# Gated linear attention on one core: the list of steps in another order, q's first piece loaded first, upper weights rounded from another tile

## The chip, the core and the metric

The kernel runs on one core of a Trainium2 chip. The core has five engines that work side by side: TensorE (PE, matrix products; PEld is its loading of weights), VectorE (DVE), ScalarE (ACT), GpSimd (POOL) and SyncE (SP), which here only issues the transfers (DMAs). Each engine takes its own instructions strictly in the order in which they were written, and waits on semaphores for what the others produce. The metric is the device time of one execution in microseconds; lower is better.

## The reference

There are 8 batches, 8 heads, 576 tokens and 64 features a head, so 512 channels. First comes linear attention, then a gated layer:

```
q_s = exp(q - max over features);  q_s = q_s / (sum over features + 1e-9)
k_s = exp(k - max over tokens);    k_s = k_s / (sum over tokens + 1e-9)
kv  = einsum('bhsd,bhse->bhde', k_s, v)
x   = einsum('bhsd,bhde->bhse', q_s, kv)          # tokens x 512 channels
gate = sigmoid(causal convolution of x over 5 tokens, one weight per tap and channel)
val  = x @ w_val
out  = (gate * val) @ w_out
```

## The kernel before

All work on x, gate, val and out is done with channels on the 128 partitions and the 576 tokens along the free axis, so a batch has four blocks of channels (0 to 3). The steps of a batch are: turning q (and for the first two batches k) so that features lie on the partitions (`q_turn`, `k_turn`, on PE; `q_turned` and `k_turned` copy the result out of PSUM); `kv`, the product of k and v, 80 short matmuls; `kv_sums` and `kv_norm`, its division by the sums; `attend b g`, which makes x for half of the blocks, 16 matmuls; `x_high` and `x_low`, which split x into a rounded upper part and the rest; `first`, `tap`, `far` with `near`, the five taps of the convolution; `sigmoid`; `value b m`, one block of val; `gated`, gate times val; `g_high` and `g_low`, the split of that; `project b n`, one block of the output; `copy` and `put`. For batch 0 the convolution of blocks 0 and 1 is done by PE (`conv`, with `conv_rows` and `conv_kv` before it).

`value` and `project` are split products of 24 matmuls of 128 x 288: lower weights by upper x, upper weights by upper x, upper weights by lower x. Weights arrive as 64-bit words and are built in pieces of a slab of 128 columns (slabs 0 to 3 of w_val, 4 to 7 of w_out): `load_words`, then `field`, `scaled`, `signed` make the upper part (tile e), `part` the lower part (tile f), `joined` adds them into f, `w_high` rounds to W hi, `w_low` subtracts to get W lo.

k's softmax has `k_sub` (subtract the maximum, four pieces and a tail) and `k_exp`; from batch 2 on, the maxima come by `load_km`, `k_peak`, `k_row`, `k_spread`. From batch 3 on the softmax of q in the turned form has `l_row` and `l_spread`, by which a row goes to memory and comes back spread over the partitions (tile lb), `l_sub` (subtract it, on tile qc) and `c_exp`.

Nothing but one list sets the order: ORDER, 973 steps written out by hand or by a planner. A loop calls each step in turn, and every engine has its instructions in this order. The last letter of a step names its engine (a ScalarE, p GpSimd, v VectorE) where there is a choice. HOMES gives for each kind of tile the buffer that its next one takes, as a string of digits, so a buffer comes free when the former tile of that digit has been read. All transfers go through SyncE's queue in the order of the list. The lines that matter below: w_high L323 and w_low L326, split_product L621, value L682, attend (matmuls L580), kv (L521), conv (L676), x_low (L600), q_max (L415), q_each (L499), k_sub (L355), k_exp (L359), l_sub (L490), near (L614).

Of the kernel before, what the change touches and what calls it, by code (L numbers as in the profile page):

```python
# [19 lines left out]
NB = C // P  # L20
# [11 lines left out]
    warm 12, load_words 3, field 3 p, load_q 0 2 5, load_kc 0 0, load_q 0 0 1, load_taps, scaled 3 p, signed 3,  # L32
    load_q 0 1 2, q_max 0 2 3, q_sub 0 2 p, q_max 0 3 5, q_sub 0 3 p, part 3 a, joined 3 v, k_top 0 0, load_ident,
    load_words 0, load_kc 0 1, load_kc 0 2, load_kc 0 3, load_words 1, load_v 0, q_max 0 0 1, tap_field p,
    tap_scaled p, tap_signed, load_vt 0, load_km 2 2, q_exp 0 2 3, q_each 0 4, q_exp 0 3 4, q_each 0 0, q_max 0 1 2,
    load_km 2 1, tap_part p, tap_joined p, diag p, q_sub 0 1 p, q_sum 0 2 5, q_eps 0 2 5 p, k_raise 0 0, q_exp 0 1 2,
    k_top 0 1, k_raise 0 1, k_turn 0 0, field 0 p, load_words 2, load_q 1 0 5, load_words 4, load_km 2 0,
    load_words 5, q_rec 0 2 5, k_top 0 2, q_mul 0 4 p, tail_turn 0, k_raise 0 2, k_top 0 3, k_raise 0 3, k_turn 0 1,
    q_sum 0 0 2, q_eps 0 0 2 a, q_mul 0 3 p, q_rec 0 0 2, load_kc 1 3, load_kc 1 0, k_turned 0 1 v, k_turned 0 0 a,
    k_tail_turn 0, k_tail_turned 0 v, q_mul 0 2 p, load_kc 1 1, field 1 p, scaled 0 a, signed 0, scaled 1 a, signed 1,  # L40
    q_mul 0 0 p, part 1 a, q_mul 0 1 a, k_peak 2 2, tail_turned 0 a, conv_rows, tail_high 0 a, joined 1 p, kv 0,
    kv_sums 0, field 2 p, kv_norm 0 v, conv_kv, load_words 7, load_kc 1 2, part 2 a, q_turn 0 0, q_turned 0 0 a,
    scaled 2 p, signed 2, joined 2 p, q_turn 0 1, q_turned 0 1 a, w_high 1 a, q_max 1 0 2, attend 0 0, w_low 1 p,
    x_high 0 1 a, x_low 0 1, x_high 0 0 a, q_sub 1 1 p, x_low 0 0, q_max 1 2 4, attend 0 1, first 0 2 a, load_words 6,
    x_high 0 3 a, load_v 1, first 0 3 a, tap 0 3 3, w_high 3 p, tap 0 3 1, part 0 a, x_high 0 2 a, field 4 p,
# [758 lines left out]
```

## Time and profile before

| | us |
|---|---|
| median of 3 runs | 287.61 (287.55 to 287.83) |
| the profiled execution | 287.65 |
| its span, first to last instruction | 285.9 |
| PE busy in it | 278.8 |
| VectorE, GpSimd, ScalarE busy | 231.7, 205.8, 192.8 |
| granted clock of PE | 1.00 of full speed throughout |

The profile comes from one execution, whose own time lies 1.75 us above its span. Times in the rows are microseconds from the first instruction. A busy time counts the instructions alone; an engine that is not busy waits, and the profile names what ended the wait.

### The profile page before, as it was taken

The page shows a single profiled execution, that of the slowest core. Times are in us where ns is not written, and L with a number is a line of the kernel's source. Part 1 is how long each engine was busy: PE and PEld are TensorE (multiplying, and loading weights), DVE is VectorE, ACT ScalarE, POOL GpSimd, SP SyncE. Part 2 cuts the span into 40 slices and gives each one's busy share as a digit, 9 for nine tenths or more (in the row PEclk, how much of TensorE's full clock was granted, in tenths as well). Part 3 has the DMA queues.
Part 4 walks back from the last instruction along what each step waited for, and adds up shares of the span by engine and source line. Part 5 has one row for each costly group of instructions (what it writes and reads, how often), then busy time and mean ns, then how long its engine had stood idle before and what let it go on. Part 6 is the DMA issues. An engine that isn't in the chain of part 4 may idle for free.

```text
span 285.9 us, 6653 instructions
## 1 busy us (share of the span) xinstructions
PE 278.8 (98%) x2640; PEld 250.6 (88%) x2640; DVE 231.7 (81%) x329; ACT 192.8 (67%) x322; POOL 205.8 (72%) x191
## 2 busy tenths in 40 slices
...
GB/s 241 397 414 399 316 226 301 214 416 346 84 262 345 250 284 128 332 198 224 371 417 257 211 225 322 287 165 126 153 182 159 217 0 2 44 41 85 0 83 85
DMA packets 23463, 62.93 MB, mean 220 GB/s; under 512 B 3432, under 2 KB 3976, under 8 KB 20744
## 3 DMA queue, kind: packets, MB, share of 16 engines
...
q8 instruction: 21, 0.34, 0.5%
q14 instruction: 10, 0.08, 0.1%
...
## 4 chain that ended last, share of the span: by engine, by line
PE 84%; DVE 7%; ACT 2%; issue 1%; POOL 1%; DVEq 0%
PE val L630 36%; PE out_a L630 32%; PE kv L521 6%; PE x L580 5%; PE cv L676 2%; DVE gate L605 2%; DVE x L600 1%; PE qTps L546 1%; DVE e L292 1%; DVE kpk L340 1%; PE kps L387 1%; ACT q L506 1%; PE out_r L630 1%; PE out_l L630 1%; POOL f L295 0%
## 5 line engine op out<-in xcount | busy, mean ns | idle before, releaser
L630 PE MATMUL val<-x,w_val_hi 128*128 128x288 f32 x512 | 89.1, 295 | 0.1
L605 DVE SCALAR_TENSOR_TENSOR gate<-x,cw,gate 128x575 f32<-128x575 f32 (+3 forms) x98 | 78.8, 809 | 5.7 <-ACT gate L593 2.2
L630 PEld LDWEIGHTS val<-x,w_val_hi 128*128 128x128 f32 x512 | 75.3, 188 | 0.3 <-DVE x L600 0.3
L630 PE MATMUL val<-x,w_val_lo 128*128 128x288 f32 x256 | 56.1, 300 | 0.0
L630 PE MATMUL out_a<-gh,w_out_lo 128*128 128x288 f32 x248 | 54.6, 301 | 0.0
L630 PE MATMUL out_a<-gh,w_out_hi 128*128 128x288 f32 x248 | 53.2, 296 | 0.0
L697 POOL TENSOR_TENSOR gl<-g,gh 128x576 fp32r<-128x576 f32 x24 | 34.6, 1443 | 14.7 <-ACT gh L198 8.0
L630 PEld LDWEIGHTS out_a<-gh,w_out_lo 128*128 128x128 f32 x248 | 39.4, 188 | 5.7 <-issue 1.8
L630 PE MATMUL out_a<-gl,w_out_hi 128*128 128x288 f32 x248 | 43.0, 295 | 0.0
L614 POOL TENSOR_TENSOR gate<-gate,far 128x572 f32<-128x572 f32 (+3 forms) x22 | 29.1, 1324 | 18.7 <-DVE gate L605 10.0
L630 PEld LDWEIGHTS val<-x,w_val_lo 128*128 128x128 f32 x256 | 40.7, 188 | 1.6 <-DVE g L689 0.4
L630 PEld LDWEIGHTS out_a<-gh,w_out_hi 128*128 128x128 f32 x248 | 39.8, 188 | 0.0
L204 ACT ACTIVATE o<-out_a 128x576 f32<-128x576 f32 x27 | 17.6, 650 | 31.6 <-PE out_a L630 22.0
L630 PEld LDWEIGHTS out_a<-gl,w_out_hi 128*128 128x128 f32 x248 | 36.4, 188 | 0.0
L420 POOL TENSOR_TENSOR q<-q,qm 128x512 f32<-128x512 f32 x32 | 33.5, 1062 | 3.6 <-DVE qm L415 3.5
L689 DVE SCALAR_TENSOR_TENSOR g<-gate,val 128x576 f32<-128x576 f32 x32 | 23.8, 749 | 13.8 <-PE val L630 5.9
L490 POOL TENSOR_TENSOR qc<-qc,lb 128x576 f32<-128x576 f32 (+1 forms) x17 | 24.1, 1428 | 11.0 <-DMA lb<-lrow 11.0
L355 POOL TENSOR_TENSOR k<-k,kmax 128x512 f32<-128x512 f32 x23 | 30.2, 1330 | 0.2
L617 ACT ACTIVATE gate<-gate 128x576 f32<-128x576 f32 x30 | 20.2, 683 | 8.3 <-DVE gate L605 8.0
L600 DVE TENSOR_TENSOR x<-x,x 128x576 fp32r<-128x576 f32 x32 | 23.1, 749 | 1.7 <-ACT x L198 1.6
L610 ACT ACTIVATE far<-x,cw 128x572 f32<-128x572 f32 (+3 forms) x22 | 16.2, 737 | 9.2 <-PE x L580 4.0
L424 ACT ACTIVATE q<-q 128x512 f32<-128x512 f32 (+2 forms) x11 | 15.9, 1442 | 8.8 <-POOL q L420 8.8
(108 smaller groups left out, 456.4 us busy)
## 6 DMA issues: line engine op xcount, KB each, us to landing
...
```

The costliest lines, as they stand in the source:

```text
L204: nc.scalar.mul(out, in_, factor)
L355: engine(e).tensor_sub(kk[r, cs], kk[r, cs], mx[r, cs])
L420: engine(e).tensor_tensor(qq, qq, m, op=ALU.add if b < 2 else ALU.subtract)
L490: engine(e).tensor_sub(t, t, T["lb", b][:, p])
L521: nc.tensor.matmul(acc[h * D:(h + 1) * D, p, :], T["k", b][:, c, cs] if c < 4 else ktz[b % 2][:, cs], T["v", b][:, c, hd] if c < 4 else T[ ...
L600: nc.vector.tensor_sub(xl, T["x", b, p], T["xh", b, p].bitcast(F32))
L605: nc.vector.scalar_tensor_tensor(out=a, in0=x, scalar=w, in1=a, op0=ALU.mult, op1=ALU.add)
L614: nc.gpsimd.tensor_add(a, a, T["far", b, p, j])
L617: nc.scalar.activation(T["gate", b, p], T["gate", b, p], AF.Tanh, scale=0.5)
L630: nc.tensor.matmul(ps[:, cs], a[:, kb, ms], z[:, cs], start=(i == 0), stop=(i == len(parts) - 1))
L689: nc.vector.scalar_tensor_tensor(out=T["g", b, m], in0=T["gate", b, m], scalar=1.0, in1=T["val", b, m], op0=ALU.add, op1=ALU.mult)
L697: engine(e).tensor_sub(T["gl", b, m], T["g", b, m], T["gh", b, m].bitcast(F32))
```

## The change

The list is written in another order, 96 of its steps go to another engine, and the buffers in HOMES are dealt anew. Both products of k and v of batches 6 and 7 stand next to an attention half. The first transfer is q's tokens 2 and 3 with the tail instead of the weights' slab 3, whose load comes later; `warm` has 11 matmuls for 12. `conv_rows` follows `warm` more closely. `w_high` rounds the upper part e of a weight, where it rounded the joined f. For batch 0 `value` takes the matmuls of the upper weights first, those of the lower weights last. By the steps' letters VectorE, ScalarE and GpSimd trade subtractions of q, k, lb and the lower g, conversions of weights and roundings; the set of matmuls, taps and transfers is the same. In the diff the lists are cut to the lines where the named steps stand.

```diff
     def w_high(i, e="a"):
-        copied(e, W[i // NB][0][:, :, slab(i)], weights(i))
+        copied(e, W[i // NB][0][:, :, slab(i)], T["e", i].rearrange("p (k c) -> p k c", k=NB))
...
-    def split_product(ps, w, hi, lo, m, order, last=0, h="a"):
+    def split_product(ps, w, hi, lo, m, order, last=0, h="a", early=False):
...
         for ks in (order[:NB - last], order[NB - last:]):
-            parts += [(w, hi[kb], kb) for kb in ks for w in (wl, wh)] + [(wh, lo[kb], kb) for kb in ks]
+            if early:
+                parts += [(wh, z[kb], kb) for z in (hi, lo) for kb in ks] + [(wl, hi[kb], kb) for kb in ks]
+            else:
+                parts += [(w, hi[kb], kb) for kb in ks for w in (wl, wh)] + [(wh, lo[kb], kb) for kb in ks]
...
-        split_product(T["val", b, m], W[0], blocks("xh", b), blocks("xl", b), m, T["split", b])
+        split_product(T["val", b, m], W[0], blocks("xh", b), blocks("xl", b), m, T["split", b], early=b == 0)
...
-    sigmoid 5 2, g_low 5 1 v, put 4 1, g_high 5 0 a, load_qc 7 1, kv 6, gated 5 2, sigmoid 5 3, l_sub 6 1 v,
-    g_high 6 1 p, gated 6 3, g_low 6 1 p, tap 6 2 1, c_exp 7 2, tap 6 2 0, g_high 6 3 p, c_exp 7 1, l_sub 7 0 p, kv 7,
-    value 7 3, gated 7 0, g_high 7 0 p, g_low 7 0 v, gated 7 3, g_high 7 3 v, g_low 7 3 v, project 7 0, project 7 1,
-    copy 7 0 a v, put 7 0, project 7 2, copy 7 1 a a, put 7 1, project 7 3 r, copy 7 2 a a, put 7 2, project 7 3 l,
...
+    tap 5 1 0, far 5 0 3, tap 5 1 2, project 4 0, load_qc 6 0, put 3 2, k_exp 6, near 5 0 3, copy 4 0 a a, attend 5 1,
+    x_high 5 2 a, x_high 5 3 v, first 5 2 a, near 5 0 0, k_peak 7 1, load_qc 7 1, first 5 3 a, far 5 2 2, q_total 6,
+    load_vt 6, kv 6, kv_sums 6, load_k 7, far 5 2 3, kv_norm 6 v, near 5 2 2, q_log 6, l_turn 6, tap 5 3 0,
+    c_exp 6 2, kv 7, l_sub 6 3 p, c_exp 6 3, tap 6 1 3, sigmoid 6 1, kv_sums 7, l_spread 7, l_sub 7 3 p, put 5 1,
+    project 7 1, copy 7 1 a a, put 7 1, project 7 3 r, copy 7 3 r v, put 7 3 r, project 7 0, copy 7 0 a a, put 7 0,
+    project 7 3 l, copy 7 3 l a, put 7 3 l,
```

SyncE's first transfers before (tile and its number, source, shape):

```order
L265 DMA words3_108<-in_w_val 128x1024
L236 DMA q0_112<-in_q 128x1024
L238 DMA q0_112<-in_q_tail 128x512
L370 DMA kc_0_0_115<-in_k_channels 128x576
L236 DMA q0_112<-in_q 128x512
L298 DMA tap_words_74<-in_conv_w 128x40
```

And SyncE's first transfers in the changed kernel:

```order
L236 DMA q0_107<-in_q 128x1024
L238 DMA q0_107<-in_q_tail 128x512
L370 DMA kc_0_0_112<-in_k_channels 128x576
L236 DMA q0_107<-in_q 128x512
L298 DMA tap_words_74<-in_conv_w 128x40
L236 DMA q0_107<-in_q 128x512
```

The slab of weights no longer stands ahead of q, and its 512 KB come after k's channels and the tail of v.

ScalarE around the end of the head before, from k's first turned copy to the first rounding of x (k0 and qT are the turned k and q, f the lower part of a weight, x2 the pair that holds x's split):

```order
L198 COPY k0_237<-kps_0_0_188 128x4x256
L204 ACTIVATE e0_197<-e0_197 128x512
L204 ACTIVATE e1_249<-e1_249 128x512
L204 ACTIVATE f1_258<-words1_142 128x512
L506 ACTIVATE q0_112<-q0_112,qs_0_181 128x64 x8
L198 COPY qTt_0_270<-qTtps_0_212 128x512
L198 COPY qT_0_277<-qTt_0_270 128x4x64
L204 ACTIVATE f2_333<-words2_199 128x512
L198 COPY qT_0_277<-qTps_0_0_335 128x2x512
L198 COPY qT_0_277<-qTps_0_1_349 128x2x512
L198 CAST w_val_hi_77<-f1_258 128x4x128
L198 CAST x2_0_1_373<-x_0_1_363 128x576
```

The same stretch of ScalarE in the changed kernel (ktz is the turned tail of k):

```order
L198 COPY k0_232<-kps_0_1_220 128x4x256
L198 COPY qT_0_244<-qTt_0_216 128x4x64
L198 COPY ktz0_83<-ktps_0_246 64x512
L198 COPY k0_232<-kps_0_0_234 128x4x256
L506 ACTIVATE q0_107<-q0_107,qs_0_176 128x64 x8
L204 ACTIVATE f1_327<-words1_127 128x512
L198 CAST w_val_hi_77<-e3_303 128x4x128
L204 ACTIVATE f2_340<-words2_165 128x512
L198 COPY qT_0_244<-qTps_0_0_329 128x2x512
L204 ACTIVATE f3_369<-words3_148 128x512
L198 COPY qT_0_244<-qTps_0_1_346 128x2x512
L198 CAST x2_0_1_385<-x_0_1_360 128x576
```

ScalarE now has both of k's turned copies and the tail's, and rounds slab 3 from its upper part e3 ahead of q's turned copies; one scaled step (e1) has left it.

GpSimd around the subtractions of k of batch 6 before (k6 and kt6 are k and its tail, qc with lb the subtraction that needs the spread row, gh and gl the split of gate times val):

```order
L490 TENSOR_TENSOR qc_5_3_2136<-qc_5_3_2136,lb5_2210 128x576
L697 TENSOR_TENSOR gl_4_2_2504<-g_4_2_2462,gh_4_2_2501 128x576
L200 CAST gh_4_1_2535<-g_4_1_2531 128x576
L697 TENSOR_TENSOR gl_4_1_2539<-g_4_1_2531,gh_4_1_2535 128x576
L614 TENSOR_TENSOR gate_5_0_2545<-gate_5_0_2545,far_5_0_3_2547 128x575
L614 TENSOR_TENSOR gate_5_0_2545<-gate_5_0_2545,far_5_0_0_2578 128x572
L355 TENSOR_TENSOR k6_2445<-k6_2445,kmax_6_2447 128x512 x2
L614 TENSOR_TENSOR gate_5_2_2631<-gate_5_2_2631,far_5_2_3_2635 128x575
L420 TENSOR_TENSOR q7_2492<-q7_2492,qm_7_2639 128x512 x4
L614 TENSOR_TENSOR gate_5_2_2631<-gate_5_2_2631,far_5_2_2_2667 128x574
L355 TENSOR_TENSOR k6_2445<-k6_2445,kmax_6_2447 128x512 x2
L355 TENSOR_TENSOR kt6_2390<-kt6_2390,kmax_6_2447 64x512
```

And GpSimd there in the changed kernel:

```order
L490 TENSOR_TENSOR qc_5_1_2088<-qc_5_1_2088,lb5_2268 128x576
L355 TENSOR_TENSOR k6_2078<-k6_2078,kmax_6_2381 128x512
L355 TENSOR_TENSOR kt6_2392<-kt6_2392,kmax_6_2381 64x512
L490 TENSOR_TENSOR qc_5_2_2398<-qc_5_2_2398,lb5_2268 128x576
L355 TENSOR_TENSOR k6_2078<-k6_2078,kmax_6_2381 128x512
L490 TENSOR_TENSOR qc_5_3_2429<-qc_5_3_2429,lb5_2268 128x576
L200 CAST gh_4_2_2466<-g_4_2_2464 128x576
L700 TENSOR_TENSOR gl_4_2_2499<-g_4_2_2464,gh_4_2_2466 128x576
L355 TENSOR_TENSOR k6_2078<-k6_2078,kmax_6_2381 128x512
L200 CAST gh_4_1_2510<-g_4_1_2505 128x576
L700 TENSOR_TENSOR gl_4_1_2512<-g_4_1_2505,gh_4_1_2510 128x576
L355 TENSOR_TENSOR k6_2078<-k6_2078,kmax_6_2381 128x512
```

The five subtractions of batch 6's k moved ahead of the near taps of batch 5 and in among the three that use lb.

## Rows read from the trace of the kernel before

**Rows 1.** The page's first section: busy us, share of span, instructions.
```profile
PE 278.8 (98%) x2640; PEld 250.6 (88%) x2640; DVE 231.7 (81%) x329; ACT 192.8 (67%) x322; POOL 205.8 (72%) x191
```

**Rows 2.** Waits of PE, the largest: total us, times, longest.
```profile
PE cv L676 <- DVE x L600: 1.1, 1, 1.1
```

**Rows 3.** Stretch 8.64:25.10: length, PE, PEld, DVE, ACT, POOL busy, clock, DMA.
```profile
8.64:25.10 16.46, 14.82 (x158) 9.01 (x156) 14.89 (x26) 16.25 (x42) 12.69 (x17) 1.00 1.03 410
```

**Rows 4.** Timeline of the head: start, us, engine, line, out<-in, count, [wait].
```profile
4.29 0.67 ACT L204 ACTIVATE f<-words 128x512 int32<-128x512 uint32 x1 [2.29 <-DMA words<-in_w_val]
...
6.80 1.80 DVE L415 TENSOR_REDUCE qm<-q 128x8 f32<-128x512 f32 x2
...
8.64 0.63 ACT L424 ACTIVATE q<-q 128x512 f32<-128x512 f32 x1 [3.68 <-POOL q L420]
...
25.50 1.19 ACT L198 CAST x<-x 128x576 fp32r<-128x576 f32 x2
25.54 1.21 DVE L415 TENSOR_REDUCE qm<-q 128x16 f32<-128x1024 f32 x1
...
26.67 1.41 DVE L600 TENSOR_TENSOR x<-x,x 128x576 fp32r<-128x576 f32 x2
...
27.47 5.73 PE L676 MATMUL cv<-qT,dg 64*64 64x288 f32 x80 [1.07 <-DVE x L600]
```

**Rows 5.** Chain of waits: start, us, engine and line.
```profile
17.18 0.90 ACT k L198
...
19.25 0.58 ACT f L204
...
42.19 3.44 PE val L630 x24
...
181.16 3.20 PE out_a L630 x24
184.36 1.13 PE x L580 x16
...
253.74 3.39 PE out_a L630 x24
...
282.75 0.41 ACT o L204
```

**Rows 6.** The page's costly groups: value's weight loads, busy, mean ns, idle before.
```profile
L630 PEld LDWEIGHTS val<-x,w_val_hi 128*128 128x128 f32 x512 | 75.3, 188 | 0.3 <-DVE x L600 0.3
```

**Rows 7.** Stretches 28.1:68.7 and 68.7:104.2, columns as in rows 3.
```profile
28.10:68.70 40.60, 40.37 (x417) 35.82 (x416) 39.98 (x58) 36.01 (x80) 33.96 (x34) 1.00 0.85 304
68.70:104.20 35.50, 35.45 (x341) 33.50 (x341) 34.64 (x47) 29.47 (x49) 32.43 (x29) 1.00 0.79 239
```

**Rows 8.** Timeline of VectorE at batch 2's last x_low.
```profile
102.77 1.41 DVE L600 TENSOR_TENSOR x<-x,x 128x576 fp32r<-128x576 f32 x2
```

**Rows 9.** Timelines of VectorE and ScalarE ahead of batch 6's k times v.
```profile
181.28 0.75 DVE L689 SCALAR_TENSOR_TENSOR g<-gate,val 128x576 f32<-128x576 f32 x1 [0.92 <-PE val L630]
...
182.07 0.67 ACT L198 CAST gh<-g 128x576 fp32r<-128x576 f32 x1 [0.80 <-DVE g L689]
...
198.41 1.92 ACT L359 ACTIVATE k<-k 128x2048 f32<-128x2048 f32 x1 [1.26 <-POOL k L355]
```

**Rows 10.** Waits of POOL, the largest: total us, times, longest.
```profile
POOL qc L490 <- DMA lb<-lrow: 11.0, 3, 5.2
```

**Rows 11.** Timelines of VectorE and GpSimd, alone and side by side.
```profile
215.17 4.44 POOL L355 TENSOR_TENSOR k<-k,kmax 128x512 f32<-128x512 f32 x3
215.19 0.75 DVE L490 TENSOR_TENSOR qc<-qc,lb 128x576 f32<-128x576 f32 x1
...
239.75 0.75 DVE L697 TENSOR_TENSOR gl<-g,gh 128x576 fp32r<-128x576 f32 x1
...
265.01 1.43 POOL L697 TENSOR_TENSOR gl<-g,gh 128x576 fp32r<-128x576 f32 x1
265.09 1.97 DVE L697 TENSOR_TENSOR gl<-g,gh 128x576 fp32r<-128x576 f32 x1 [0.77 <-POOL gh L200]
```

More of the change, by code (lines that the diff above doesn't have):

```diff
@@ L31 @@
 ORDER = [step.strip() for step in """
[L32 to L45, printed above, removed]
-    tap 0 3 0, q_each 1 3, conv, field 5 p, x_low 0 3, scaled 5 p, tap 0 3 2, joined 0 p, w_high 0 p, w_low 0 p,
@@ L137 @@
[L137 to L139 removed]
+    warm 11, load_q 0 2 5, q_max 0 2 3, load_kc 0 0, q_sub 0 2 p, load_q 0 0 1, load_taps, load_q 0 1 2, load_ident,
+    load_kc 0 1, load_words 0, load_kc 0 2, load_kc 0 3, load_words 1, tap_field p, load_v 0, load_vt 0, q_max 0 3 5,
@@ new lines @@
+    tap 1 0 1, joined 6 p, w_high 6 a, load_km 5 2, q_sub 2 2 p, project 0 1, copy 0 1 a a, put 0 1, part 7 a,
+    tap 1 1 0, tap 1 0 0, tap 1 0 3, w_low 6 p, k_spread 2, project 0 0, copy 0 0 a a, q_sub 2 4 p, tap 1 1 3,
+    attend 1 1, first 1 3 a, x_high 1 3 a, q_sub 2 3 p, x_high 1 2 a, project 0 2, x_low 1 1, q_sub 2 1 p, tap 1 1 1,
+    tap 1 1 2, signed 7, sigmoid 1 1, w_high 7 p, far 1 2 2, joined 7 p, q_sub 2 0 v, load_km 3 3, first 1 2 a,
+    x_low 1 3, x_low 1 2, w_low 7 p, tap 1 3 2, k_sub 2 1 p, value 1 0, k_sub 2 3 p, tap 1 2 3, k_sub 2 4 p, put 0 0,
@@ new lines @@
+    q_sub 5 1 p, project 2 2, copy 2 2 a a, attend 3 1, far 3 3 1, x_high 3 2 v, l_row 4, k_sub 4 3 v, x_high 3 3 a,
+    first 3 2 a, tap 3 2 3, q_sub 5 3 p, put 2 1, first 3 3 a, x_low 3 3, x_low 3 2, tap 3 2 2, project 2 3,
+    value 3 0, k_exp 4, copy 2 3 a a, kt_exp 4, kv 4, near 3 3 1, q_sub 5 2 p, tap 3 3 0, tap 3 3 2, far 3 2 1,
+    tap 3 2 0, sigmoid 3 0, gated 3 0, tap 3 3 3, value 3 2, q_sub 5 0 p, load_qc 4 0, q_exp 5 0 4, q_total 5,
+    q_log 5, k_row 5, k_peak 6 3, k_peak 7 0, near 3 2 1, sigmoid 3 2, g_high 3 0 p, g_low 3 0 p, sigmoid 3 1,
@@ new lines @@
+    x_high 4 0 a, l_sub 4 2 v, tap 4 1 3, c_exp 4 2, project 3 3, k_sub 5 0 p, x_low 4 0, x_high 4 1 a, tap 4 0 3,
+    x_low 4 1, c_exp 4 3, kt_exp 5, q_max 6 0 5, k_sub 5 1 p, copy 3 3 a a, project 3 1, copy 3 1 a a, near 4 1 0,
+    tap 4 0 0, k_exp 5, attend 4 1, x_high 4 3 a, first 4 2 v, tap 4 2 2, tap 4 2 0, x_high 4 2 a, x_low 4 2,
+    l_spread 5, tap 4 2 1, near 4 1 1, x_low 4 3, project 3 2, q_sub 6 1 p, q_sub 6 4 p, q_sub 6 0 p, value 4 0,
+    q_sub 6 3 p, put 3 3, q_sub 6 2 v, load_qc 5 0, copy 3 2 a a, tap 4 2 3, l_sub 5 0 v, sigmoid 4 0, kv 5,
```

198 lines of the change are left out of this document (97 added, 101 removed).

## Prediction

> **What bounds the kernel now.** I read the page first: TensorE (PE) is busy 278.8 of 285.9 us, the next engine, VectorE, 231.7 [rows 1]. Then the waits of PE: the largest is 1.1 us, once, for VectorE's subtraction that splits x into its upper and lower part (L600) [rows 2]. Then the timeline of the head: from 27.47 on the convolution runs, its main part once that wait is over at about 28.1 (x_low of the first two blocks runs from 26.67 to 28.08) [rows 4]. Behind it PE stands almost without a gap up to 282.72, where the copy of the last product begins [rows 5]. So the matmuls, of which the change has the same set, set the time between 28.1 and 282.7, and an edit can act in four places only: how early the convolution starts; how long a product takes beside its neighbours; the small waits inside; the last microseconds. The two engines that feed PE are nearly full at the start: ScalarE is busy 16.25 of 16.46 us between 8.64 and 25.10 [rows 3], VectorE 39.98 of 40.60 in the stretch behind it [rows 7]. Only later is there slack.
>
> **The head.** Before, the first load is a slab of weights (512 KB); q's tokens 2 and 3 come second and q's tail third. The weights are used at 4.29, when they have landed, and the maxima of the q that came behind them begin at 6.80 [rows 4]: 768 KB more in 2.5 us, some 300 GB/s. ScalarE's first exponential of q starts at 8.64 [rows 4]. After, q's 512 KB go first and will be there at about 4.3, the tail's 256 KB 0.85 later, at 5.15. One maximum over two pieces takes 1.21 [rows 4], so ScalarE can start on the tail at about 6.4, 2.2 us earlier, without the subtraction on GpSimd in between.
>
> But ScalarE has more to do from there to the end of q's last turned copy (q_turned 0 1; before it ended the stretch of [rows 3], at 25.1). New ahead of it are k's turned copy of the other half (0.90, the row of such a copy [rows 5]), two part steps (2 x 0.58 [rows 5]), the rounding of an upper weight (bounded by the same 0.58; it reads and writes as much), the turned tail of k (as much again) and two tiny ones, put at 0.27; one scaled step leaves, priced by the part's 0.58. The sum is 0.90 + 1.16 + 0.58 + 0.58 + 0.27 - 0.58 = 2.9. ScalarE was full, so this comes on top: q_turned 0 1 ends at 25.1 - 2.2 + 2.9 = 25.8. Its two roundings of x take 1.19 together [rows 4], so they end at 27.0. The subtraction of the first block then starts at about 26.4 rather than 26.67, once VectorE's maximum of batch 1 (25.54, 1.21 [rows 4]) is done; that maximum gets free of the weight step that stood ahead of it, by about 0.6, so it ends at 26.1 and does not decide. The second subtraction starts at 27.05 and ends at 27.75, against 28.08. I take -0.4. At best ScalarE's additions hide elsewhere and VectorE's maximum decides, which is 0.6 earlier: -0.6. At worst the tail comes late and only 1.2 of the 2.2 are there: q_turned 0 1 ends at 26.8, the second subtraction at 28.7, so +0.6.
>
> The granted clock is 1.00 in the head, with PE busy 14.82 of 16.46 [rows 3]. The new head gives PE no pause that I work out as longer than 1.6 us (18 to 19.5, k's copies), so I put nothing on the clock.
>
> **The seams.** A product (24 matmuls) takes 3.20 behind another product, and 3.39 to 3.44 behind an attention half, a k times v or a turn of q or k: the chain of waits has the first such at 42.19 and the last at 253.74, and a plain one at 181.16 [rows 5]. By the written order there are 23 such places before and 21 after: k times v of batches 1, 6 and 7 move next to another short piece (-3), and k's turn of batch 1 is split by a product (+1). That is 2 x 0.19 = 0.4. What a seam between k times v and an attention half costs isn't seen in the trace before; it lies between nothing and the 0.19 of the seam that goes. I take nothing, so -0.4, with bounds of 0 and -0.6.
>
> **The wait inside.** Weight loads of the value products wait 0.3 us for x_low in one place, value of batch 1 [rows 6]. Between x_low of the last block of batch 0 and the one that is waited for, VectorE has by the rows of its own steps 37.5 us of work after the change, 39.6 before, in a stretch where it is full [rows 7]. So 2 us of slack come, and the wait goes: -0.3.
>
> **The upper weights rounded early.** w_high reads the upper part directly, so it need not wait for the join. For batch 0 the matmuls with the lower weights come last, 2.1 us (16 of 24 matmuls of a 3.20 product) behind the first. In the rows of PE's waits no weight stands ahead of x_low [rows 2, 6], so there is nothing to give back: nothing. What covers it is that the matmuls with the new W lo now come last; were w_high late instead, its product would wait, which the same rows don't bound.
>
> **Batches 6 and 7.** k times v of batch 6 goes some 20 us earlier. What it needs is k_exp 6, which stood at 198.41 for 1.92 [rows 9], right ahead of the old place. In the new order ScalarE comes to it behind the rounding of g of batch 4's last block and one far tap: that block's g began at 181.28 and took 0.75 [rows 9]. PE is 0.7 ahead there by the head and the wait inside, so g ends at 181.3, the rounding (0.67) and far (priced by the same 0.67 [rows 9]) at 182.65, and k_exp at 184.6. PE comes to the new place, behind a product (3.20) and an attention half (1.13) that began at 181.16 [rows 5]: 181.16 - 0.7 + 4.3 = 184.8. So there is no margin; if the far tap's own input or GpSimd's subtraction before k_exp is late, the wait is up to the 1.26 that k_exp waited for GpSimd before [rows 9]. Between 0 and 1.3 I take 0.4. v's tail and k come by DMA with about as little to spare. For batch 7 the gap is some 4 us between the last load and its use: nothing.
>
> **Engines.** 96 steps change their engine. By the durations of each step's rows VectorE gets 7 us more, ScalarE 5.5 more, GpSimd 25 less. VectorE's 231.7 [rows 1] become some 239 of 286, still behind PE's; it costs only where VectorE is full [rows 7], which is rival B.
>
> **The tail.** The last products change places but the last one to be copied is the same left half of block 3 (0.41 at 282.75 [rows 5]), with one 288 KB store more in the queue ahead of it, started 1.4 us earlier: nothing, at most 0.2.
>
> **The sum**: -0.4 (head) - 0.4 (seams) - 0.3 (wait) + 0.4 (batch 6) = -0.7 on the profiled execution's 287.65 (span 285.9 and 1.75 around it), which is 0.04 over the median 287.61 of the runs. That gives 286.9.
>
> **One rule of the skill against this.** VectorE's subtraction of the lower g took 0.75 at 239.75 while GpSimd was idle, but 1.97 at 265.09 when GpSimd had one of 1.43 since 265.01; yet at 215.19 one took 0.75 beside GpSimd's three that began at 215.17 and took 1.48 each [rows 11]. The Trainium skill, "GPSIMD Engine Reference", section "8. Key points", says that GpSimd shares its SBUF interfaces with VectorE and that it contends with VectorE instructions that have two SBUF inputs. The first pair agrees, the second only in that GpSimd's is the one that is stretched. By that rule the 15 steps with two such inputs that VectorE gets would be paid for twice where both engines work.
>
> **The rivals.**
> A. *The head gives nothing*: ScalarE's 2.9 us eat the 2.2, VectorE or GpSimd is late instead. For it: [rows 3], no slack. Against: VectorE's maximum moves up. Without the head's 0.4 the sum is -0.3: 287.35, no change. 0.20.
> B. *VectorE is stretched beside GpSimd*, by up to 1.2 us an instruction as at 265.09 [rows 11]. The place is x_low of batch 2's last blocks, which ends at 104.18 before [rows 8]. From x_low of batch 1 up to there VectorE's steps come to 37.2 us after, 34.7 before, where it is busy 34.64 of 35.50 [rows 7]: 2.5 more, of which 0.9 fits the idle time and the rest waits unless the product has slack there, so 0 to 1.6. I take 0.9: 286.95 + 0.9 = 287.85. Against: GpSimd has 25 us less to disturb it with. 0.15.
> C. *Slower: batch 6's k times v is too early.* k_sub 6 stands on GpSimd behind the step on qc of batch 5 that needs the rows lb from memory; GpSimd waited for these 11.0 us in 3 places before, 5.2 the longest [rows 10]. If that or the load of v's tail is late, k_exp 6 ends late and PE stands with nothing behind it able to pass. It decides once PE's wait passes 1.6, with k_exp 6 ending after 186.4. As its price I take half the longest, 2.6, less the margin of 0.2: 2.4 in place of the 0.4 of the sum, 286.95 + 2.0 = 288.95. 0.17.
> D. *Both terms at their best and nothing given back at batch 6*: 287.65 - 0.6 - 0.6 - 0.3 = 286.15, taken as 286.1. 0.06.
> That the change does not do what it says is left with 0 of weight, since the order of each engine shows it.
>
> **How the numbers follow.** Forecast 0.42, A 0.20, B 0.15, C 0.17, D 0.06. About 0.2% (0.58 us) is what a measurement of this kernel can tell from no change: faster is below 287.03, slower above 288.19. The forecast lies only 0.1 inside, so of its 0.42 I give 0.32 to faster and 0.10 to the same; with D (0.06) and a rest of A and B on the faster side (0.07) faster is 0.45. The same is 0.10 + 0.16 (A) + 0.08 (B) = 0.34; slower is C (0.17) with 0.04 of B = 0.21. The likeliest case's own range is 286.3 to 287.2; the range that should hold 8 in 10 goes from D's 286.1 to within 0.4 of C's, 288.6.
>
> **What would show it.** Right: the convolution's main run starts at 27.5 to 27.9; the weight-load wait for x_low of batch 1 is gone; k times v of batch 6 waits under 1 us for ScalarE; the tail from the last product on takes 3.2. Wrong: a PE wait of more than 1 us behind 28 that has no counterpart before, on k_exp 6 (C) or on x_low of batch 2 (B); a convolution that starts at 28 or later (A).

## The result, and the profile after

The changed kernel is slower: 291.6 us (290.27 to 292.87, 4 runs) against 287.72 for the kernel before in the same comparison, a ratio of 1.0133 (95% interval 1.0105 to 1.0161). Its own runs lie 2.6 us apart, those of the kernel before 0.5. The profiled execution is the slowest of the four: 292.87, span 291.1. The forecast was 286.9, with a range up to 288.6. A ratio, here and in the table of experiments, leaves out runs more than 1.5% above the fastest of their own kernel, while medians and ranges have all runs; the two part clearly only for after_back, where four of six are left out.

First the page, its first section and the row of PE's clock (tenths of full speed in 40 slices), answering [rows 1]:

```profile
PE 281.4 (97%) x2638; PEld 252.2 (87%) x2638; DVE 241.8 (83%) x345; ACT 196.7 (68%) x332; POOL 185.5 (64%) x165
...
PEclk9998999999999999999999999999999999999999
```

PE has 2.6 us more busy time with the same matmuls but one in `warm`, and one slice near the start with less clock. PE's waits (us in total, times, longest), answering [rows 2]:

```profile
PE kv L521 <- ACT k L198: 1.6, 1, 1.6
PE warm L730 <- POOL ones L748: 1.0, 1, 1.0
PE x L580 <- DVE kvd L537: 1.0, 2, 0.7
...
PE out_a L633 <- POOL gl L700: 0.7, 1, 0.7
...
PE val L633 <- DVE x L600: 0.3, 1, 0.3
```

The convolution's wait of 1.1 is gone; four others have come. Where they cost is read by setting each PE step's start against that of the same step before. The changed kernel is late by 1.56 us at the end of the convolution (34.76, before 33.20); by 1.47 at the second attention half of batch 2 (99.39, 97.92); by 4.27 at project 2 1 (126.63, 122.36); by 5.30 at project 3 3 (158.58, 153.28); by 5.61 at the second half of batch 5 (189.90, 184.29); by 5.22 at the end (287.93, 282.71). So there are three places of loss: the head, 97 to 127, and 149 to 175. Behind them the kernel gains.

**The head.** Timeline of PE before and in kv of batch 0:

```profile
17.79 0.60 PE L399 MATMUL ktps<-ident,kc 128*64 128x128 f32 x4
19.97 0.73 PE L521 MATMUL kv<-v,k 128*64 128x65 f32 x16 [1.58 <-ACT k L198]
...
20.70 1.09 PE L521 MATMUL kv<-v,k 128*64 128x65 f32 x16
```

PE stood 1.58 us for ScalarE's second copy of k and began kv 0. Its first 16 matmuls took 0.73, the next 16 took 1.09; before, such 16 took 0.64. The granted clock of the stretch falls (length; PE, PEld, DVE, ACT, POOL busy; clock; DMA):

```profile
18.40:24.10 5.70, 4.13 (x81) 4.07 (x82) 4.25 (x9) 5.09 (x14) 1.85 (x2) 0.70 1.03 406
```

A mean of 0.70 is a mixture of the two levels, 2.4 and 1.2 GHz; kv 0 took 4.13 instead of 2.55. That is as much as the head's 1.56; the rest of the head comes out even, since kv 0 begins 0.42 later than before and the convolution's wait of 1.1 is gone. The matching timeline of ScalarE, VectorE and PE, answering [rows 4]:

```profile
5.00 2.02 DVE L415 TENSOR_REDUCE qm<-q 128x8 f32<-128x512 f32 x2 [5.00 <-DMA q<-in_q]
...
7.06 2.02 ACT L499 ACTIVATE q<-q,qm 128x64 f32<-128x64 f32 x8 [5.05 <-DVE qm L415]
...
17.15 0.99 ACT L198 COPY k<-kps 128x1024 f32<-128x1024 f32 x1
18.43 0.58 ACT L198 COPY ktz<-ktps 64x512 f32<-64x512 f32 x1
18.91 1.00 ACT L198 COPY k<-kps 128x1024 f32<-128x1024 f32 x1
```

q's first piece is there at 5.0, ScalarE starts 1.6 earlier than before (7.06, 8.64), and then has all three of k's copies one behind the other.

**97 to 127.** SyncE's issues of batch 3's row (lrow, lb) and of k of batch 4, before:

```profile
93.82 0.79 SPq L475 DMA_DIRECT2D lrow<-lt  x1
...
97.15 1.33 SPq L486 DMA_DIRECT2D lb<-lrow  x2
...
100.99 0.42 SPq L226 DMA_DIRECT2D k<-in_k  x1
```

and after:

```profile
99.06 0.79 SPq L475 DMA_DIRECT2D lrow<-lt  x1
99.91 0.39 SPq L226 DMA_DIRECT2D k<-in_k  x1
103.47 1.32 SPq L486 DMA_DIRECT2D lb<-lrow  x2
```

The row comes 5 us later, and k's megabyte now stands between its two transfers. The chain of waits from there (start, us, what):

```profile
99.06 4.33 DMA lrow<-lt
...
103.47 8.87 DMA lb<-lrow
...
116.17 1.31 POOL qc L490
...
118.05 0.61 ACT qT L493
118.66 0.59 ACT gate L617
...
119.33 0.75 DVE g L692
120.08 0.23 DVE kvd L537
```

and what GpSimd did meanwhile, with PE's wait behind it:

```profile
107.09 1.41 POOL L614 TENSOR_TENSOR gate<-gate,far 128x572 f32<-128x572 f32 x1
114.93 2.54 POOL L490 TENSOR_TENSOR qc<-qc,lb 128x512 f32<-128x512 f32 x2 [6.43 <-issue]
117.42 2.83 POOL L700 TENSOR_TENSOR gl<-g,gh 128x576 fp32r<-128x576 f32 x2
```
```profile
126.26 0.53 PE L633 MATMUL out_a<-gl,w_out_hi 128*128 128x288 f32 x2 [0.69 <-POOL gl L700]
```

One late transfer holds three queues: GpSimd's first qc stands idle for 6.4 us with g's lower parts behind it, ScalarE's c_exp with a sigmoid behind it, and VectorE's gated with kv_norm behind that. Attention of batch 3 and project 2 0 wait; the latter takes 5.10 instead of 3.47. These two are 1.9 of the 2.8 lost here; 0.66 went earlier, at value 2 1, which waits for x_low.

**149 to 175.** Attention of batch 4 begins 0.7 later still, for kv_norm 4 (kvd). In this execution VectorE does not wait for a transfer ahead of it; it is full. Busy times from batch 3's first attention half to batch 4's (columns as above, VectorE the third after the length), after and before:

```profile
121.77:153.85 32.08, 30.58 (x288) 28.67 (x289) 30.95 (x45) 22.88 (x32) 25.51 (x21) 1.00 0.73 223
```
```profile
119.12:148.85 29.73, 29.73 (x289) 28.56 (x289) 24.42 (x34) 20.91 (x28) 27.55 (x24) 1.00 0.92 295
```

VectorE has 6.5 us more to do there than before, 30.95 of 32.08. Two of its rows after:

```profile
147.02 1.90 DVE L355 TENSOR_TENSOR k<-k,kmax 128x512 f32<-128x512 f32 x1
...
153.28 0.42 DVE L537 TENSOR_TENSOR kvd<-kv,ks 128x256 f32<-128x256 f32 x1
```

The subtraction of k, one of the steps moved to VectorE, stands ahead of kv_norm 4; it took 1.90 here and 0.68 in a second profile (run again below).

**Behind 175 us** the order does what it should. The chain there:

```profile
189.97 1.13 PE x L580 x16
191.10 2.48 PE kv L521 x80
```

kv of batch 6 follows the attention half without a wait. Behind kv 6 and kv 7 the lateness falls from 5.61 to 5.22: two seams of 0.2.

### The profile page after: what moved, and what is told of

Its sections match the earlier page's. It is cut to its first block, busy times and chain, and to the rows that moved or that the text cites. A ratio compares the mean times of both kernels' runs of the same rounds, so it can differ in the third digit from the quotient of the medians.

```text
span 291.1 us, 6636 instructions
## 1 busy us (share of the span) xinstructions
PE 281.4 (97%) x2638; PEld 252.2 (87%) x2638; DVE 241.8 (83%) x345; ACT 196.7 (68%) x332; POOL 185.5 (64%) x165
## 4 chain that ended last, share of the span: by engine, by line
PE 64%; DVE 17%; DMA 7%; ACT 6%; issue 4%; POOL 1%; SPq 0%; DVEq 0%; POOLq 0%; ACTq 0%
PE out_a L633 26%; PE val L633 25%; PE kv L521 6%; DVE gate L605 5%; PE x L580 4%; DMA lb<-lrow 3%; DMA lrow<-lt 2%; DVE qs L449 2%; DVE x L600 2%; PE qTps L546 2%; DVE qm L415 2%; DMA q<-in_q_tail 2%; ACT q L499 1%; DVE k L355 1%; DVE g L692 1%
## 5 line engine op out<-in xcount | busy, mean ns | idle before, releaser
L633 PE MATMUL val<-x,w_val_hi 128*128 128x288 f32 x512 | 87.7, 297 | 0.5 <-DVE x L600 0.3
L605 DVE SCALAR_TENSOR_TENSOR gate<-x,cw,gate 128x573 f32<-128x573 f32 (+3 forms) x98 | 77.8, 809 | 4.2 <-POOL gate L614 1.2
L633 PEld LDWEIGHTS val<-x,w_val_hi 128*128 128x128 f32 x512 | 74.5, 188 | 1.6 <-DVE x L600 0.5
L633 PE MATMUL val<-x,w_val_lo 128*128 128x288 f32 x256 | 53.7, 298 | 0.0
L700 POOL TENSOR_TENSOR gl<-g,gh 128x576 fp32r<-128x576 f32 x20 | 29.5, 1480 | 16.4 <-DVE gh L200 9.5
L420 POOL TENSOR_TENSOR q<-q,qm 128x512 f32<-128x512 f32 x27 | 28.6, 1083 | 9.3 <-DVE qm L415 9.3
L490 POOL TENSOR_TENSOR qc<-qc,lb 128x576 f32<-128x576 f32 (+1 forms) x14 | 19.4, 1402 | 17.4 <-DMA lb<-lrow 9.0
L355 POOL TENSOR_TENSOR k<-k,kmax 128x512 f32<-128x512 f32 x22 | 29.4, 1350 | 0.4 <-DMA kmax<-krow 0.2
L415 DVE TENSOR_REDUCE qm<-q 128x8 f32<-128x512 f32 (+3 forms) x12 | 20.9, 1741 | 5.1 <-DMA q<-in_q 5.0
L593 ACT ACTIVATE gate<-x,cw 128x576 f32<-128x576 f32 x27 | 19.6, 743 | 6.1 <-PE x L580 6.1
```

The lines of the kernel that those rows point to most:

```text
L355: engine(e).tensor_sub(kk[r, cs], kk[r, cs], mx[r, cs])
L415: nc.vector.tensor_reduce(out=T["qm", b][:, cs], in_=qq, axis=AX.X, op=ALU.max, negate=b < 2)
L420: engine(e).tensor_tensor(qq, qq, m, op=ALU.add if b < 2 else ALU.subtract)
L490: engine(e).tensor_sub(t, t, T["lb", b][:, p])
L593: nc.scalar.activation(a, x, AF.Copy, scale=w)
L605: nc.vector.scalar_tensor_tensor(out=a, in0=x, scalar=w, in1=a, op0=ALU.mult, op1=ALU.add)
```

## The experiments

All times are medians in us; the kernel before lay between 287.72 and 287.86 in each comparison. The ratio is to it.

| run | what | median (range) | ratio, 95% interval |
|---|---|---|---|
| again | the changed kernel | 292.06 (290.13 to 294.9) | 1.0148 (1.0112 to 1.0184) |
| lb_first | k's load behind lb | 289.65 (288.69 to 291.1) | 1.0067 (1.0044 to 1.0091) |
| before_k_ahead | before, k's load ahead of lb | 287.88 (287.61 to 288.49) | 1.0005 (0.9996 to 1.0013) |
| before_bunched | the same with more loads behind k_row 3 | 287.85 (287.65 to 288.09) | 1.0000 (0.9991 to 1.0008) |
| norm | lb_first, kv_norm 4 early | 287.82 (287.26 to 291.11) | 1.0023 (0.9997 to 1.0049) |
| puts | lb_first, two stores early | 288.31 (287.93 to 290.56) | 1.0046 (1.0024 to 1.0067) |
| all_three | norm and puts | 288.48 (287.57 to 291.46) | 1.0036 (1.0013 to 1.0060) |
| kcopy_dve | changed, two copies of k on VectorE | 294.58 (291.36 to 296.1) | 1.0211 (1.0173 to 1.0250) |
| pause | norm, one copy on VectorE | 288.60 (288.1 to 290.1) | 1.0035 (1.0019 to 1.0051) |
| head | pause, ScalarE relieved | 290.03 (289.08 to 291.67) | 1.0087 (1.0058 to 1.0116) |
| pause_long | norm, longer pause | 290.17 (289.4 to 291.14) | 1.0087 (1.0069 to 1.0105) |
| pause_act | norm, copies reordered | 288.33 (287.38 to 290.5) | 1.0023 (1.0003 to 1.0043) |
| after_pause | changed, copies reordered | 289.97 (288.14 to 292.55) | 1.0078 (1.0048 to 1.0109) |
| best | pause_act, value 2 1 relieved | 288.62 (286.75 to 291.1) | 1.0021 (1.0003 to 1.0039) |
| back_two | pause_act, two subtractions on GpSimd | 287.73 (287.43 to 289.38) | 1.0005 (0.9993 to 1.0017) |
| back_all | pause_act, twelve on GpSimd | 291.74 (291.08 to 293.86) | 1.0127 (1.0111 to 1.0142) |
| after_back | changed, twelve on GpSimd | 295.62 (290.78 to 297.13) | 1.0167 (1.0115 to 1.0218) |
| best_two | back_two and best | 288.07 (286.73 to 291.95) | 1.0009 (0.9988 to 1.0030) |

**again** has no edit.

> The changed kernel once more, unchanged. Both theories: median 290.3 to 292.9 as before. What differs between its own runs is to be seen: if TensorE's fall to the lower clock level at 20.5 to 23.9 belongs to every run, the time from kv 0 on is again 1.6 us longer; if not, kv of batch 0 takes 2.5 and not 4.1, and the loss before batch 3 (kv 0 to conv) is near 0 while the 2.0 at project 2 0 stays.

In this profile kv 0 follows the same pause of 1.58 and takes 2.5 at full clock; the convolution ends at 33.49, 0.3 behind the kernel before. So the head's 1.56 is not in every run. But another wait is there, which the first profile did not have:

```profile
100.04 0.65 ACT L204 ACTIVATE o<-out_a 128x576 f32<-128x576 f32 x1 [3.41 <-DMA out<-o]
```
```profile
100.74 0.54 PE L633 MATMUL out_a<-gh,w_out_lo 128*128 128x288 f32 x2 [2.31 <-ACT o L204]
```
```profile
101.70:105.20 3.50, 3.50 (x17) 3.50 (x17) 3.46 (x6) 3.18 (x5) 3.50 (x4) 0.51 0.85 312
```

A store that took 7 us to land held its buffer, the copy and PE for 2.3 us, and then PE ran at the lower level (0.51). What waits, and whether the clock falls, differs between runs of one program. The two waits of the first profile are there no more: lb is late again (GpSimd's qc begins at 111.51, behind 4.6 idle), but PE is 3.2 late by then and stands neither at project 2 0 nor at batch 4. So the losses do not add up. That small margins are what the runs have in common is a reading, not a result.

**lb_first**

```diff
-    first 2 3 a, load_k 4, k_peak 6 1, k_peak 6 2, l_spread 3,
+    first 2 3 a, k_peak 6 1, k_peak 6 2, l_spread 3, load_k 4,
```

> The changed kernel with one step moved: the load of k of batch 4 (1 MB) behind the two transfers that spread the row of batch 3 (lb), as in the kernel before. Theory (the megabyte stands ahead of lb in the DMA engines): lb lands in 5 to 6 us instead of 8.9, project 2 0 takes 3.4 instead of 5.1, attend 3 0 waits no more, and the time falls by 2.0 us. Rival (VectorE and GpSimd have too much work there, whoever waits): lb lands earlier, the time stays within 0.5 us.

2.4 less, where 2.0 was expected, and the intervals do not meet: the theory holds. GpSimd's first qc begins at 108.70 instead of 114.93, and project 2 0 waits no more. The old place of the load is a risk and not a fixed cost, though: five profiled executions have it ahead of lb, and qc begins at 114.93 (the first), 111.51 (again), 114.69 (kcopy_dve), 109.90 (after_pause) and 116.69 (after_back); PE loses 1.9, 0, 1.9, 0 and 3.4 at attend 3 0 and project 2 0. **before_k_ahead** and **before_bunched** ask the reverse.

```diff
-    l_row 3, project 1 0,
+    l_row 3, load_k 4, project 1 0,
```

> The kernel before with one step moved: the load of k of batch 4 ahead of the transfers of lb of batch 3. Theory (1 MB ahead of lb): lb of batch 3 lands 3 to 4 us later, GpSimd waits for it ahead of two g_low of batch 2, and PE loses 1 to 2 us at project 2 0, so 288.7 to 289.7. Rival (the loss comes from the engines' work in the new order): within 0.4 of 287.6.

> The kernel before with the load of k of batch 4 ahead of lb, and also three loads of batch 4's k maxima (0.9 MB) and the store of block 2 of batch 0 behind k_row 3, as the changed kernel has them. Theory (bunched transfers are enough by themselves): 288.3 to 290. Rival (they matter only with the thinner margins of the new order on GpSimd, ScalarE and VectorE): within 0.4 of 287.7, as in before_k_ahead.

(before_bunched also has load_km 4 3, 4 2, 4 1 and put 0 2 behind k_row 3.) Both: no change, the rivals hold. In before_k_ahead lb took up to 9.3 us, but GpSimd's qc began at 108.96, as before (108.99), because there the subtractions of q 4 and k 3 stood ahead of it, 7.6 us of work:

```profile
101.41 5.07 POOL L420 TENSOR_TENSOR q<-q,qm 128x512 f32<-128x512 f32 x5
106.42 2.60 POOL L355 TENSOR_TENSOR k<-k,kmax 128x512 f32<-128x512 f32 x2
108.96 2.56 POOL L490 TENSOR_TENSOR qc<-qc,lb 128x512 f32<-128x512 f32 x2
```

Taken together, the late transfer seems to cost only since the new order starts the row 5 us later and has no work left ahead of its use; no run moves the row alone, so this is argued and not shown.

**norm**

```diff
-    k_row 5, k_peak 6 3,
+    k_row 5, kv_sums 4, kv_norm 4 v, k_peak 6 3,
```

> lb_first with one more pair of steps moved: kv_sums 4 and kv_norm 4 on VectorE ahead of k_sub 5 2, which waits for kmax of batch 5 from memory (landed 11.3 us after its issue). Theory (VectorE's own order: the wait of one instruction for a transfer holds kv_norm, and PE waits for it at attend 4 0): PE's 0.9 there and 0.2 to 0.3 behind it go, the time falls by 1.0 to 1.3 us against lb_first. Rival (project 3 0 is then late for g_high and g_low on the same engine): 0 to 0.4 less.

1.8 less by the median, and by the median the time of the kernel before; 3 of its 11 runs are late (289.62 to 291.11), and its interval just meets that of lb_first. In the two profiles the edit's own part is 0.9: from attend 4 0 to project 3 3 lb_first loses 1.27, norm 0.35. What it took away is seen in lb_first's chain:

```profile
133.11 11.30 DMA kmax<-krow
...
144.50 1.30 DVE k L355
...
150.17 0.44 DVE kvd L537
...
150.74 1.20 PE x L580 x16
```

A subtraction of k, which the change had moved to VectorE, waits 1.0 for kmax; kv_norm stands behind it, and PE waits 0.9 at batch 4. In the changed kernel's first profile the same subtraction did not wait; there VectorE's work alone held kv_norm. Moving kv_norm ahead takes away both.

**puts** (on lb_first) and **all_three** (on norm)

```diff
-    k_peak 3 3, k_row 3, ... put 0 2, ... put 0 3,
+    k_peak 3 3, put 0 2, put 0 3, k_row 3,
-    k_peak 6 1, k_peak 6 2, l_spread 3, ... x_low 2 2, x_low 2 3,
+    l_spread 3, ... x_low 2 2, x_low 2 3, k_peak 6 1, k_peak 6 2,
```

> lb_first with the stores of batch 0's blocks 2 and 3 ahead of k_row 3 on SyncE's queue (as in the kernel before, where they are not behind the burst of loads), and k_peak 6 1, 6 2 on VectorE behind x_low 2 2, 2 3. Theory (5 MB of transfers let go at once behind k_row 3: a store lands late, its buffer holds up the copy and so PE at project 1 1; and VectorE's x_low 2 3 is late by 0.7): the two waits, 0.8 to 2.3 and 0.66, go and the time falls by 1.4 to 2.5 us against lb_first. Rival (the store is not what holds the copy): only the 0.66 goes.

> Both of the edits of norm and puts on lb_first. Theory: all of the loss from 97 to 155 us goes, the seams (0.4), the 0.3 at value 1 0 and the head stay as in the changed kernel, so 286.0 to 287.0, under the kernel before. Rival (the clock or VectorE takes it back elsewhere): 287.7 or more.

puts is 1.3 faster than lb_first by the median, with intervals that overlap. In its profile the wait at project 1 1 is away, but norm's, without the edit, has none either; and value 2 1 keeps its 0.66. all_three is not faster than norm, against its theory. Inconclusive: these waits come and go between runs.

**kcopy_dve, pause, head, pause_long, pause_act, after_pause** ask about PE's pause before kv 0.

```diff
 kcopy_dve:
-    k_turned 0 1 a, ... k_tail_turned 0 a,
+    k_turned 0 1 v, ... k_tail_turned 0 v,
 pause (on norm):
-    tail_high 0 a, k_tail_turn 0, k_tail_turned 0 a, k_turned 0 0 a, kv 0, ... q_mul 0 0 v,
+    k_tail_turn 0, k_turned 0 0 a, tail_high 0 a, ... q_mul 0 0 v, k_tail_turned 0 v, kv 0,
 head (on pause):
-    w_high 3 a, part 2 a, ... part 3 a, ... x_high 0 2 a,
+    part 2 a, ... x_high 0 2 a, part 3 a, w_high 3 a,
 pause_long (on norm):
-    k_turned 0 0 a, kv 0, ... part 1 a,
+    part 1 a, k_turned 0 0 a, kv 0, ...
 pause_act (on norm), after_pause (on the changed kernel):
-    tail_high 0 a, k_tail_turn 0, k_tail_turned 0 a, k_turned 0 0 a, kv 0,
+    k_tail_turn 0, k_turned 0 0 a, k_tail_turned 0 a, tail_high 0 a, kv 0,
```

> The changed kernel with two copies of k of batch 0 (k_turned 0 1 and k_tail_turned 0) back on VectorE. Theory (ScalarE's serial copies make the pause of 1.6 us before kv 0): kv 0 starts at about 19.2 instead of 19.97, the pause is 0.8, PE keeps the upper clock level, and the time falls by 0.7 to 2.3. Rival (VectorE, not ScalarE, sets the start of the convolution): the pause gets shorter but conv starts when it did, time within 0.4.

> norm with the pause of PE before kv 0 cut: the tail of k is copied by VectorE and q's tail copied after k's second half, so kv 0 starts at about 19.1 instead of 20.2 (pause 0.7 instead of 1.58). Theory (in some runs the pause of 1.6 us is followed by 3.4 us at TensorE's lower clock level, as in the profile of the changed kernel, and those are norm's runs at 289.6 to 291.1): no run above 288.5, median 286.9 to 287.5, spread under 0.6. Rival (these runs are late for transfers that land late in the middle): one run in four stays 2 us above the rest.

> pause, and ScalarE does part 3 and the rounding of slab 3 (1.2 us) behind x_high of batch 0's first blocks instead of ahead of q_turned 0 1. Theory (ScalarE's extra 2.9 us set the convolution's start, as the prediction's head has it): the convolution starts 0.6 to 1.2 earlier than in norm (27.70) and the time is 286.2 to 286.9, below the kernel before. Rival (VectorE's own steps set it): start and time as in pause.

> norm with the pause before kv 0 made longer: ScalarE does part 1 (0.6 us) ahead of k's second copy, so PE stands 2.2 us instead of 1.58. Theory (the longer pause brings the lower clock level in more runs): most or all runs at 290 or more, against 3 of 11 of norm; in the profile kv 0 takes 4.1. Rival (other causes): the median moves by 0 to 0.6 alone and the share of late runs stays.

> norm with ScalarE's three copies before kv 0 in another order (k's second half, then k's tail, then q's tail), no work moved to another engine: kv 0 starts about 1 us earlier and PE's pause before it is 0.7 instead of 1.58. Theory (the pause brings TensorE's lower clock level in about a quarter of the runs; pause was slower only since VectorE got the copy): no run above 288.5, median 287.0 to 287.6, convolution not later than 27.7. Rival (late runs come from transfers): one run in four stays at 289.6 or more.

> The changed kernel with only that new order of three copies. Theory: median 0.4 to 1.2 under the changed kernel's 291.6 to 292.1, no lower level at kv 0; the waits for lb and kmax remain, so still 290 or more, and PE's pause at project 1 1 can still bring the lower level. Rival (the head is not part of the loss): within 0.3 of it.

kcopy_dve cut the pause to 0.7 and lost 2.5 us: VectorE's steps on weights came later, ScalarE's w_high 3 waited 1.15 for them, with q's copies behind it, and the convolution began at 29.51, where again has 27.76; both of its expectations missed. 4 of its 6 runs have a granted clock of 0.987 to 0.994, so part of the 2.5 is the clock. pause (only the tail's copy moved) had the convolution at 28.18 against norm's 27.70; head, with ScalarE relieved, still at 28.08, and its time is 1.4 longer than that of pause. The expectation that ScalarE sets the start fell: in both the convolution waits for VectorE's x_low, 0.64 and 0.69, and VectorE is busy 10.65 of the 11.00 us from 17 to 28. pause_long's six runs all lie above 289.3, and its profile has the lower level again, with kv 0 at 4.07:

```profile
20.81 1.13 PE L521 MATMUL kv<-v,k 128*64 128x65 f32 x16 [2.13 <-ACT k L198]
```

Its median is 2.35 above norm's; in the profile 1.5 of that is kv 0 at the lower level and 0.6 its later start. Two of its six runs (289.40 and 290.34) have a granted clock of 1.000, so the clock is not all of it.

pause_act has the pause cut without new work for VectorE, and the convolution at 27.18, half a us earlier than norm. Yet 6 of its 12 runs lie above 288.5. So the theory that norm's late runs come from this pause does not hold for all of them. The granted clock of each run tells the two kinds apart: every profiled execution in which PE works for a stretch at the lower level has a mean of 0.992 or 0.993, every other 0.998 or more. Of norm's three late runs two have 0.994, of pause_act's six only one; the other five are late at full clock. On the changed kernel the same edit is worth 2.1 (289.97 against 292.06), more than the 0.4 to 1.2 expected, with ranges that overlap. Its profile (288.31, one of its lowest) has no loss at project 2 0, though k's load is ahead of lb there too.

**back_two, back_all, after_back.** pause_act's profiled execution, 289.44 and so one of its late ones, has on VectorE:

```profile
166.97 1.75 DVE L420 TENSOR_TENSOR q<-q,qm 128x512 f32<-128x512 f32 x1
...
169.38 2.49 DVE L490 TENSOR_TENSOR qc<-qc,lb 128x576 f32<-128x576 f32 x1
...
174.42 0.42 DVE L537 TENSOR_TENSOR kvd<-kv,ks 128x256 f32<-128x256 f32 x1
```

and on GpSimd beside it:

```profile
166.88 1.30 POOL L355 TENSOR_TENSOR k<-k,kmax 128x512 f32<-128x512 f32 x1 [0.28 <-DMA kmax<-krow]
...
169.85 1.40 POOL L490 TENSOR_TENSOR qc<-qc,lb 128x576 f32<-128x576 f32 x1
```

while norm's (287.63), which differs there by 0.3 us, has on VectorE and GpSimd:

```profile
166.67 0.68 DVE L420 TENSOR_TENSOR q<-q,qm 128x512 f32<-128x512 f32 x1
...
168.00 1.12 DVE L490 TENSOR_TENSOR qc<-qc,lb 128x576 f32<-128x576 f32 x1
```
```profile
166.99 1.50 POOL L355 TENSOR_TENSOR k<-k,kmax 128x512 f32<-128x512 f32 x1 [0.42 <-DMA kmax<-krow]
```

In norm VectorE's q began first (166.67, GpSimd's next at 166.99); in pause_act GpSimd began 0.09 us ahead and VectorE's took 1.07 more. The second, begun at 169.38 while GpSimd was in a subtraction since 168.13, lasted until 0.62 after GpSimd's next one had ended. The pair costs 2.4 in all, kv_norm 5 comes late and PE waits 1.2 at batch 5. The profile of pause has the same (1.63 and 2.48, 1.0 at batch 5). back_two sends these two back to GpSimd; back_all and after_back all twelve such subtractions of q, k and lb of batches 2 to 7.

```diff
-    q_sub 6 2 v, ... l_sub 5 0 v,
+    q_sub 6 2 p, ... l_sub 5 0 p,
```

> pause_act with two subtractions (q_sub 6 2 and l_sub 5 0) back on GpSimd. In its profile they took 1.75 and 2.49 us on VectorE, alone 0.68 and 0.75, each beside a GpSimd instruction that had begun just before, and kv_norm 5 and attend 5 0 waited 1.2 behind them; in norm's profile the same two took 0.68 and 1.12. Theory (VectorE instructions with two inputs in SBUF are held by GpSimd, differently in each run): the upper half of pause_act's runs (288.6 to 290.5) falls under 288.5, median 287.4 to 287.8. Rival (late runs are late for transfers): half the runs stay above 288.5.

> pause_act with all twelve subtractions of q, k and lb of batches 2 to 7 that stand on VectorE back on GpSimd (about 15 us more for GpSimd). Theory: spread under 0.6, median 287.2 to 287.7. Rival (GpSimd then runs late itself, its queue being in order): a median of 288.5 or more, with PE waiting for kvd or x.

> The changed kernel with only these twelve subtractions back on GpSimd. Theory (the wait for kmax of batch 5 at the head of VectorE's queue is also gone, since k_sub 5 2 is one of them): 1.0 to 2.0 under 291.6 to 292.1, the loss by lb of batch 3 stays. Rival (their place does not matter): within 0.5.

back_two: 287.73, 0.6 under pause_act, with 3 of 12 runs above 288.5 and no loss at batch 5 in its profile: the median is as the theory had it, but not every run, and the intervals overlap. back_all is 3.4 slower than pause_act: GpSimd's own queue then runs late (attention of batch 6 waits 1.7 for qT). So the moves to VectorE are needed by the new order, and paid for. after_back's median is 3.6 above the changed kernel's, but its interval overlaps that of again, so it adds nothing sure; the gain that its theory expected is not there.

**best** and **best_two**

```diff
-    tap 2 2 2, kt_exp 3, ... first 2 3 a, k_peak 6 1, k_peak 6 2, l_spread 3, ... x_low 2 2, x_low 2 3,
+    tap 2 2 2, ... first 2 3 a, kt_exp 3, l_spread 3, ... x_low 2 2, x_low 2 3, k_peak 6 1, k_peak 6 2,
```

> pause_act, with k_peak 6 1, 6 2 behind x_low 2 3 on VectorE and kt_exp 3 behind first 2 3 on ScalarE, which x_low 2 3 waited for at 104.5 in all_three. Theory: the 0.66 at value 2 1 falls to 0.2 or less; 286.5 to 287.2, below the kernel before (287.7). Rival: VectorE's maximum of q of batch 4 (2.8 us) is what holds x_low 2 3, 0.1 or less is gained on pause_act.

> back_two with the two edits of best (k_peak 6 1 and 6 2 behind x_low 2 3, kt_exp 3 behind first 2 3), which took the 0.66 at value 2 1 away in best's profile. Theory (the forecast's terms are all there once the waits are undone): most runs at 286.7 to 287.3, median 0.5 under the kernel before. Rival (VectorE's stretched instructions leave other waits in other runs): the lowest runs reach 286.8, the median stays at 287.6 to 288.

In both profiles value 2 1 has no wait left, and in best's PE ends at 282.37, 0.34 before that of the kernel before (that execution's own time, 287.83, lies 2.3 above its span and not 1.75). The lowest runs are 286.75 and 286.73, as forecast; the medians are not. In best_two's profile the store is late again:

```profile
PE out_a L633 <- ACT o L204: 0.9, 1, 0.9
```

No version beats the kernel before: back_two's median is 0.13 below it, at a ratio of 1.0005 whose interval holds 1.

## Why the prediction was wrong

- *The seams*: right. Two seams less behind kv 6 and kv 7 are 0.4 of the lateness between 185 and 257 us, as [rows 5] gave it. At batch 1, where the forecast had them at nothing (kv 1 less, k's turn more), PE gained 0.6 in again, lb_first and norm: k's turn, split by products, took 2.1 of PE's time in place of 2.5. That was not foreseen; it is luck.
- *The wait inside*: right. Between attend 1 1 and kv 2 the kernel gains 0.3.
- *Batch 6*: the given-back 0.4 was not there; kv 6 waits for nothing, in norm, where PE is on time, as little as in the changed kernel.
- *The head*: the -0.4 was not found in the changed kernel's two profiles. It was also reckoned from the wrong end. The row of the convolution in [rows 4] begins at 27.47 and its 80 matmuls take 5.73 without a stop, so it waited for the first x_low alone (26.67 and 0.75); that the second ended at 28.08 held nothing up. Its start of 27.5 to 27.9, named as a sign of being right, is thus no gain, and again's 27.76 is 0.3 late. ScalarE starts 1.6 earlier and not 2.2, since q landed at 5.0 and not at 4.3 and there are two maxima, done at 7.0. Without the fall of the clock the convolution ends 0.3 later than before (again); rival A's "the head gives nothing" is what happened there. In the profiled execution it cost 1.56, 1.28 of it more than in again, with kv 0 at the lower level. The sentence "I put nothing on the clock" was wrong: the pause was worked out, 1.6, and taken to be harmless because the stretch before had shown 1.00. That stretch had no single pause longer than 0.9.
- *The step that failed is "Engines"*, with the claim that what leaves PE's path costs only where VectorE is full. It counted busy time by engine over the whole kernel (VectorE came to 241.8, some 239 were forecast), looked for a full VectorE at batch 2 alone, and did not ask what stands ahead of what in each queue. Two orders decided: load_k 4 ahead of l_spread 3 on SyncE (2.4 by the medians), and k_sub 5 2, now on VectorE, ahead of kv_norm 4 (1.8). Behind each stands work that PE needs: behind the row lb that comes late, and behind a VectorE that is full (30.95 of 32.08 us, first profile) or waits for kmax (1.0, lb_first). Undone, the median is that of the kernel before, while some runs stay late. What the forecast counted as gains is there early on: at batch 2's first attention half PE is 0.75 to 1.1 ahead of the kernel before in again, lb_first, norm, puts and all_three, and loses it again behind 97.
- *Rival C* had this mechanism, a queue held by lb, but at batch 5 and with kv 6 as its victim. It was priced at +2 and came at batch 3, with project 2 0 as the victim. I checked the rows that wait most [rows 10], and not the batches where the new order leaves least time.
- *Rival B* named the right mechanism too. At its place, value 2 1, the wait was 0.66 and not 0.9; best's profile loses it by moving kt_exp 3 and the two peaks, so a queue was its cause at least in part. The stretching [rows 11] did its harm at batch 5, in some runs. The Trainium skill, "GPSIMD Engine Reference", section "8. Key points", has GpSimd contend with VectorE instructions that have two SBUF inputs; the trace agrees in the pair 166.88 and 166.97, and the engine that starts second is the one that takes longer.
- *The range* was too narrow, since it came from single costs, and here several of them came together.

What stays open: the share of late runs. back_two has 3 of 12 above 288.5, best_two still has runs of 290.7 to 292.0, and no profile was taken of such a run. The granted clock singles out some: 0.994 in best_two's 290.71 and in two of norm's three late runs; best_two's 291.51 and 291.95 have 1.000. Late stores and stretched instructions are seen in single profiles; which of them makes the late runs at full clock isn't shown, nor why some executions lie 2.3 to 2.9 above their span, where the kernel before lies 1.7 to 1.9.
